# Half of batch 2's q and k taken to their turned form by DMA instead of by TensorE and VectorE

## The chip, the cores and the metric

The kernel runs on one core of one Trainium2 chip. The metric is the device time of one execution in microseconds (us); the time of a kernel is the median of its runs. The engines are called as the profile calls them: PE is TensorE's matmul side, PEld its weight load, DVE is VectorE, ACT is ScalarE, POOL is GpSimd, SP is SyncE, which here only issues DMAs.

## The reference

Eight batches of eight heads, 576 positions, head width 64. `f` is a forget gate per position; its logarithms are summed along the sequence, and the differences of the sums are added to the causal attention scores. The attention output, laid out as 4608 tokens by 512, goes through an MLP.

```python
scores = scale * q @ k^T + (cum[:, :, :, None] - cum[:, :, None, :])   # causal, scale = 1/8
attn = softmax(scores)            # cum = cumsum(log(clip(f, 1e-4, 1)))
x = (attn @ v).transpose(0, 2, 1, 3).reshape(4608, 512)
h = x @ w_in                      # 512 x 2048
out = (h - tanh(h)) @ w_out       # 2048 x 512
```

## The kernel before

All work is in fp16 with fp32 accumulation. The engines' orders are written out by hand: each engine runs its instructions in the order in which the program emits them, and waits in that order.

**Slots.** The work goes by pairs of heads: pair p is batch p // 4, heads 2(p % 4) and 2(p % 4) + 1. Batch 0 has a stage of its own at the start (`scores0`, `values0`). From then on there is one slot per pair, p = 4 to 32 (`slot`, L628). Slot p emits seven score tiles (`scores`, L349, called s0 to s6 here: scores in PE, exponent in ACT, from batch 2 on a causal mask in POOL), the product with v of the pair before it (`values`, L382, after s1), the transposing DMAs of that product's result into XR (`turn`, L400, on SP's queue) and between them a number of MLP steps given by TAKE (L745). An MLP step is four to eight matmuls: `mlp1` gives 128 rows of h for 512 tokens and its gate (ACT tanh L416, DVE add L417), `mlp2` (L577) and `seven` (L520) are the second product. XR is a ring of three batches.

**q and k.** A score needs q and k with the head width on the partitions: QT[b % 2] and KT[b % 2], 64 rows of values and 3 rows that carry the decay (`load_aug`, L168). How they come there differs by batch:

- Batches 1 and 2 (b < FAR, L18): `load_qk` (L213) brings whole rows to the raw tiles qn and kn, six positions to a partition. In slot p, for the pair p + 1, `trans` (L247) makes six PE transposes for q (L256) and two DVE copies to QT (L265), and the same for k (L616 and L620 place them). Each row run is 768 bytes in the raw tile.
- Batches 3 to 7: `load_heads` (L102) brings blocks of 128 positions, five per tensor, with 128 bytes per position and head. `turn_all` (L108) turns the whole tile into TQ or TK by one transposing DMA of 22 blocks of 128 x 128, and `place` (L111) copies from there to QT or KT, one DMA for the even heads (a = 0) and one for the odd ones (a = 1). `turn_all` and `place` are issued by SP, the loads by POOL.

**The table LOADS** (L218 to L238) says after which score tile of which slot a load, a turn or a place is emitted: the key (p, ti) means slot p, behind tile ti. For batch 3 the q loads are in slot 7, the k loads in slot 8, the turn of q at (8, 4), of k at (9, 4), the places of q at (9, 5) and (9, 6), of k at (10, 5) and (10, 6). Slot 12 is the first to use them. v of batch 2 is loaded in slot 5.

So around the change SP's queue holds, in this order: the XR turns of slot 7, a store of the MLP, three decay rows for batch 3 (`load_aug(3)` at (8, 0)), the XR turns of slot 8, a store, the turn to TQ, a store, the XR turns of slot 9, a store, the turn to TK, the places of q, and so on.

**Raw tiles.** Each of qn and kn has two, raw[x][0] for even batches and raw[x][1] for batch 1 and 3; after batch 3 raw[x][1] holds sums of weights for the later MLP. Columns that no load fills must hold finite numbers before a tile is turned; memsets see to that (L155 on DVE at the start, L221 on POOL in slot 5).

Of the kernel before, what the change touches and what calls it, by code (L numbers as in the profile page):

```python
# [14 lines left out]
PITCH = 640  # L15
VW = 66
SHIFT = 5.0
FAR = 3  # L18
# [4 lines left out]
def kernel(  # L23
# [10 lines left out]
    nc = tc.nc  # L34
    P = 128

    B, H, S, D = q.shape
# [4 lines left out]
    NPAIR = H // 2  # L42
    NJ = 5
    AW = D + 4
    NT6 = 6
    RW = H * S * D // (S // NT6)
# [30 lines left out]
    HH = H // 2  # L77
    raw = [[qkp.tile([P, RW], FP16, tag=f"{x}n{i}", name=f"{x}n{i}") for i in range(2)] for x in "qk"]
    qn, kn = ([t[0:S // NT6, :].rearrange("p (h n d) -> p h n d", h=H, n=NT6) for t in ts] for ts in raw)
    qa, ka = (t[0][:, 0:NJ * H * AW].rearrange("p (n h d) -> p n h d", n=NJ, h=H) for t in raw)  # L80
    HP, LEAD = NJ * D, 2 * P
    TC = NPAIR * PITCH + LEAD
# [5 lines left out]
    QT = [qkp.tile([D + 3, H, S], FP16, tag=f"QT{i}", name=f"QT{i}") for i in range(2)]  # L88
    KT = [qkp.tile([D + 3, H, PITCH], FP16, tag=f"KT{i}", name=f"KT{i}") for i in range(2)]
    TQ = qkp.tile([P, TC], FP16, tag="TQ", name="TQ")  # L90
    TK = qkp.tile([P, TC], FP16, tag="TK", name="TK")

    def load_block(dst, src, b, n, h0=0, h1=H):
        pn = min(P, S - n * P)
        nc.gpsimd.dma_start(out=dst[0:pn, n, h0:h1, 0:D], in_=src[b, h0:h1, n * P:n * P + pn, :].rearrange("h p d -> p h d"))  # L95
# [3 lines left out]
        nc.gpsimd.dma_start(out=dst[p0:P, n, :, 0:D],  # L99
                            in_=src[0, :, n * P:(n + 1) * P - p0, :].rearrange("h p d -> p h d"))  # L100

    def load_heads(dst, src, b, n):  # L102
        pn = min(P, S - n * P)
        to = dst[0:pn, n * P:n * P + D]
        to = bass.AP(to.tensor, to.offset, [list(to.ap[0]), [HP, H], [1, D]])
        nc.gpsimd.dma_start(out=to, in_=src[b, :, n * P:n * P + pn, :].rearrange("h p d -> p h d"))  # L106

    def turn_all(dst, src):  # L108
        nc.sync.dma_start_transpose(out=dst.rearrange("p (x t) -> p x t", t=P), in_=src[:, 0:TC])

    def place(dst, src, b, a):  # L111
        of = src[a * D:(a + 1) * D, a * LEAD:a * LEAD + NPAIR * PITCH].rearrange("d (c s) -> d c s", s=PITCH)
        nc.sync.dma_start(out=dst[b % 2][0:D, a:H:2, 0:S], in_=of[:, :, 0:S])

    def load_v(b, n):
        load_block(vn[b % 2], v, b, n)

    def raw_of(b):
        return 1 if b == FAR else 0
# [32 lines left out]
    nc.vector.memset(vn[0][D:P, NJ - 1, :, 0:D], 0.0)  # L152
    nc.vector.memset(KT[0][:, :, S:PITCH], 0.0)
    for one, _ in raw:
        nc.vector.memset(one[3 * P // 4:P, NJ * H * AW:TC], 0.0)  # L155
    first = cst.tile([1, 1], FP32)

    def logs(c0, c1):
# [9 lines left out]
    def load_aug(b):  # L168
        i, h0 = b % 2, b * H
        nc.sync.dma_start(out=KT[i][D:D + 1, :, 0:S], in_=chi[h0:h0 + H, :])  # L170
        nc.sync.dma_start(out=QT[i][D + 2:D + 3, :, :], in_=cq[h0:h0 + H, :])
        nc.sync.dma_start(out=KT[i][D + 1:D + 2, :, 0:S], in_=clo[h0:h0 + H, :])
# [36 lines left out]
    def load_wout(t0, t1):  # L209
        nc.gpsimd.dma_start(out=wout[:, t0:t1, :],  # L210
                            in_=moe_w_out[t0 * P:t1 * P, :].rearrange("(t p) e -> p t e", p=P))

    def load_qk(dst, src, b, h0, h1):  # L213
        nc.gpsimd.dma_start(
            out=dst[b % 2][:, h0:h1, :, :].rearrange("p h n d -> p h (n d)"),
            in_=src[b, h0:h1, :, :].rearrange("h (p n) d -> p h (n d)", n=NT6))

    LOADS = {(NPAIR, 5): [lambda: load_qk(qn, q, 2, 0, H)],  # L218
             (NPAIR, 6): [lambda: load_qk(kn, k, 2, 0, H)]}
    for _, two in raw:  # L220
        LOADS.setdefault((2 * NPAIR - 3, 5), []).append(lambda two=two: nc.gpsimd.memset(two[3 * P // 4:P, 0:TC], 0.0))  # L221
    for i in range(2 * HF):
        LOADS.setdefault((2 * NPAIR + 3 + i // 4, i % 4 * 2), []).append(lambda i=i: weight_sums(i))
    for b in range(2, B):
        p0 = (b - 1) * NPAIR
        for n in range(NJ):
            LOADS.setdefault((p0 + 1, n), []).append(lambda b=b, n=n: load_v(b, n))
        LOADS.setdefault((p0, 0), []).append(lambda b=b: load_aug(b))
        if b < FAR:
            continue  # L230
        for n in range(NJ):
            LOADS.setdefault((p0 - 1, n), []).append(lambda b=b, n=n: load_heads(raw[0][raw_of(b)], q, b, n))
            LOADS.setdefault((p0, n), []).append(lambda b=b, n=n: load_heads(raw[1][raw_of(b)], k, b, n))
        LOADS.setdefault((p0, 4), []).append(lambda b=b: turn_all(TQ, raw[0][raw_of(b)]))
        LOADS.setdefault((p0 + 1, 4), []).append(lambda b=b: turn_all(TK, raw[1][raw_of(b)]))
        for n, (dst, src) in enumerate(((QT, TQ), (KT, TK))):
            for a in range(2):
                LOADS.setdefault((p0 + 1 + n, 5 + a), []).append(lambda b=b, dst=dst, src=src, a=a: place(dst, src, b, a))  # L238
# [194 lines left out]
    def weight_sums(i):  # L433
        what, x = divmod(i, HF // 2)
        lo, hi = slice(2 * x, 2 * x + 2), slice(HF + 2 * x, HF + 2 * x + 2)
        b11, b12, b21, b22 = (wout[:, r, c] for r in (lo, hi) for c in (slice(0, HD), slice(HD, DM)))
        t2x = t2[x // 2][:, x % 2 * 2:x % 2 * 2 + 2, :]
        out, in0, in1 = ((t1[:, lo, :], b12, b11), (t2x, b22, t1[:, lo, :]),
                         (t3[:, lo, :], b22, b12), (tn4[:, lo, :], b21, t2x))[what]
        nc.vector.tensor_tensor(out=out, in0=in0, in1=in1, op=ALU.subtract)  # L440
# [163 lines left out]
    def att_items(p):  # L604
        items = []
        here = pairs[p] if p < len(pairs) else None
        before = pairs[p - 1] if NPAIR < p else None
        after = pairs[p + 1] if p + 1 < len(pairs) else None
        for ti in range(len(TILES)):
            if here:  # L610
                items.append((lambda ti=ti: scores(*here, ti), "s%d" % ti))
            for load in LOADS.get((p, ti), ()):
                items.append((load, ""))
            late = 2 * (p == 2 * NPAIR - 1)
            if ti == late and after and after[0] < FAR:
                items.append((lambda: trans(*after, qn, QT, "AV" if after[0] == 1 else "VV"), "q"))  # L616
            if ti == 1 and before:
                items.append((lambda: (values(*before), turn(*before)), "v"))
            if ti == 3 + late // 2 and after and after[0] < FAR:
                items.append((lambda: trans(*after, kn, KT, "VV"), "k"))  # L620
        return items

# [96 lines left out]
        load_v(1, n)  # L719
    load_qk(qn, q, 1, HH, H)  # L720
    load_qk(kn, k, 1, HH, H)
    for t in range(0, NFT, 4):
        load_wout(t, t + 4)
    scores0(3, 5)
# [54 lines left out]
```

## Time and profile before

| | |
|---|---|
| median of 3 runs | 348.85 us (348.4 to 349.51) |
| the profiled execution | 347.78 us |
| its span, first to last instruction | 346.1 us |
| granted TensorE clock | 0.998 |
| PE busy | 335.8 us (97%) |
| DVE, ACT, POOL busy | 236.3, 222.6, 156.1 us (68%, 64%, 45%) |
| DMA, 16 engines, first 28 of 40 slices | 0.9 or more, nearly all |

The profile is of one execution. A row of the timeline gives the start in us, how long the group took, the engine, the line of the kernel, the operation, out<-in, how often, and in brackets the idle time before it and what ended it. SPq rows are DMA issues: their length is the time that SP spends on the issue, not that of the transfer. Matmuls overlap, so PE's real pace is read from start to start.

Slots can be read from PE's rows: slot 7 begins at 54.4 us, slot 8 at 61.4, slot 9 at 72.9, slot 10 at 83.8, slot 11 at 93.7 and slot 12 at 102.9.

### The profile page before, as it was taken

To read this page: it belongs to the slowest core of one execution; us is meant where nothing else is said; L and a number is where in the kernel's file an instruction comes from. 1 tells how busy PE (TensorE), PEld (TensorE's weight loads), DVE (VectorE), ACT (ScalarE), POOL (GpSimd) and SP (SyncE) were. 2 spreads that over 40 slices of the span, in tenths; PEclk is the share of its full clock that TensorE was granted. 3 is DMA by queue.
4 is the path that set the end of the run, shared out by engine and by line. 5 is a ranking of instruction groups with operands and counts; after the bars stand their busy time and mean duration, and the time that the engine had idled before them with its cause. 6 is when DMAs were issued, how large, how long until landed. Compare 5 with 4: busy or idle time off the path is not lost.

```text
span 346.1 us, 8718 instructions
## 1 busy us (share of the span) xinstructions
PE 335.8 (97%) x3384; PEld 235.9 (68%) x3384; DVE 236.3 (68%) x481; ACT 222.6 (64%) x417; POOL 156.1 (45%) x293
## 2 busy tenths in 40 slices
PE   6889999999999999999999999999999999999995
PEld 3779886555555557888886568656887786486485
DVE  6587888447953598558764885378637865975973
ACT  4777886448755786578757875587568843623631
POOL 8973664655277626664586548652222210000000
PEclk9999999999999999999999999999999999999999
DMA  9999999999999999999999989999330013012002
GB/s 85 139 199 189 204 183 163 157 185 180 166 120 131 203 177 153 120 172 157 172 179 205 163 168 169 196 184 159 81 111 19 17 50 110 0 33 91 0 32 91
DMA packets 161324, 45.96 MB, mean 133 GB/s; under 512 B 141507, under 2 KB 159235, under 8 KB 161283
## 3 DMA queue, kind: packets, MB, share of 16 engines
q0 software_dynamic: 100128, 18.36, 77.2%
q1 hardware_dynamic: 61074, 26.99, 40.0%
q8 instruction: 26, 0.43, 0.5%
q14 instruction: 16, 0.12, 0.1%
q10 hardware_dynamic: 80, 0.07, 0.1%
HBM read 36.85 MB, written 9.44 MB: 134 GB/s over the span
## 4 chain that ended last, share of the span: by engine, by line
PE 87%; DVE 5%; ACT 4%; DMA 2%; issue 1%; ACTq 0%; DVEq 0%
PE hps L464 31%; PE cx L505 14%; PE cz L505 10%; PE ps L360 10%; PE ops L583 8%; PE av L388 7%; PE hps L450 3%; DMA XR<-xn 2%; PE ps L302 1%; ACT e L307 1%; DVE gt L417 1%; DVE KT L265 1%; PE t L274 1%; ACT th L416 1%; ACT e L369 1%
## 5 line engine op out<-in xcount | busy, mean ns | idle before, releaser
L464 PE MATMUL hps<-XR,win 128*128 128x512 f16 (+4 forms) x640 | 125.9, 336 | 1.1 <-DMA XR<-xn 0.8
L417 DVE TENSOR_TENSOR gt<-hps,th 128x512 f16<-128x512 f32 x144 | 98.4, 688 | 39.7 <-ACT th L416 38.5
L369 ACT ACTIVATE e<-ps 128x512 f16<-128x512 f32 x168 | 98.4, 594 | 40.4 <-PE ps L360 37.4
L416 ACT ACTIVATE th<-hps 128x512 f32<-128x512 f32 x144 | 86.1, 598 | 29.8 <-PE hps L464 20.9
L379 POOL TENSOR_SCALAR_AFFINE_SELECT e<-e 128x128 f16<-128x128 f16 x144 | 49.3, 343 | 99.1 <-ACT e L369 98.1
L464 PEld LDWEIGHTS <-win 128*128 128x128 f16 x640 | 56.3, 97 | 43.7 <-issue 0.5
L360 PE MATMUL ps<-QT,KT 67*128 67x512 f16 (+1 forms) x336 | 69.8, 277 | 0.8 <-ACT e L369 0.5
L505 PEld LDWEIGHTS <-gt 128*128 128x128 f16 x560 | 52.5, 97 | 8.3 <-DVE gt L417 0.4
L360 PEld LDWEIGHTS <-KT 67*128 67x128 f16 x336 | 32.2, 98 | 22.7 <-issue 1.4
L95 POOL DMA_DIRECT2D vn<-in_v_dram x40 | 34.1, 856 | 9.9 <-PE ps L363 1.7
L583 PE MATMUL ops<-wout,gt 128*128 128x512 f16 x128 | 32.5, 378 | 0.0
L388 PEld LDWEIGHTS <-e 128*128 128x128 f16 x784 | 28.0, 97 | 3.3
L498 DVE TENSOR_TENSOR snap<-cz,snap 128x512 f32<-128x512 f32 x21 | 14.5, 691 | 22.4 <-PE cz L505 7.4
L388 PE MATMUL av<-vn,e 128*128 128x65 f16 x784 | 29.2, 193 | 0.0
L505 PE MATMUL cz<-wout,gt 128*128 128x256 f16 x224 | 27.8, 272 | 0.0
L106 POOL DMA_DIRECT2D qn<-in_q_dram x25 | 21.2, 850 | 6.0 <-PE ps L363 3.4
L396 DVE TENSOR_TENSOR xn<-av,rs 128x640 f16<-128x640 f32 x28 | 23.1, 825 | 1.0
L505 PEld LDWEIGHTS <-sw 128*128 128x128 f16 x224 | 21.1, 97 | 3.9
L106 POOL DMA_DIRECT2D kn<-in_k_dram x25 | 21.3, 853 | 1.3 <-issue 1.3
L542 ACT ACTIVATE snap<-cx 128x512 f32<-128x512 f32 (+1 forms) x16 | 8.7, 544 | 16.2 <-PE cx L505 16.2
L583 PEld LDWEIGHTS <-gt 128*128 128x128 f16 x128 | 11.0, 97 | 10.0
L307 ACT ACTIVATE e<-ps 128x512 f16<-128x512 f32 x25 | 14.3, 596 | 4.6 <-PE ps L305 2.5
(108 smaller groups left out, 385.6 us busy)
## 6 DMA issues: line engine op xcount, KB each, us to landing
vn<-in_v_dram POOLq DMA_DIRECT2D x32, 128.0 KB, 7.1
out_dram<-ost SPq DMA_DIRECT2D x14, 256.0 KB
out_dram<-snap SPq DMA_DIRECT2D x14, 256.0 KB
qn<-in_q_dram POOLq DMA_DIRECT2D x24, 128.0 KB, 5.3
kn<-in_k_dram POOLq DMA_DIRECT2D x24, 128.0 KB, 4.8
QT<-TQ SPq DMA_DIRECT2D x10, 288.0 KB
KT<-TK SPq DMA_DIRECT2D x10, 288.0 KB
win<-in_moe_w_in_dram POOLq DMA_DIRECT2D x2, 1024.0 KB, 11.1
```

Source lines behind the costliest of these rows:

```text
L95: nc.gpsimd.dma_start(out=dst[0:pn, n, h0:h1, 0:D], in_=src[b, h0:h1, n * P:n * P + pn, :].rearrange("h p d -> p h d"))
L106: nc.gpsimd.dma_start(out=to, in_=src[b, :, n * P:n * P + pn, :].rearrange("h p d -> p h d"))
L360: nc.tensor.matmul(out=ps[:, col:col + n], lhsT=KT[b % 2][0:D + 3, h, j * P:(j + 1) * P], rhs=QT[b % 2][0:D + 3, h, i0:i0 + n], start=True ...
L369: nc.scalar.activation(out=e[:, lo:hi], in_=ps[:, lo:hi], func=AF.Exp, scale=qscale)
L379: nc.gpsimd.affine_select(out=view, in_=view, compare_op=ALU.is_ge, fill=0.0, base=0, pattern=pat, channel_multiplier=-1)
L388: nc.tensor.matmul(out=av[:, a, ib, :], lhsT=E.pop((b, 2 * c + a, j, ib)), rhs=vn[b % 2][:, j, 2 * c + a, 0:D + 1], start=(j == 0), stop=( ...
L396: nc.vector.tensor_tensor(out=xn.rearrange("p i (a d) -> p a i d", a=2), in0=av[:, :, :, 0:D], in1=rs.to_broadcast([P, 2, NJ, D]), op=ALU. ...
L416: nc.scalar.activation(out=th, in_=hps, func=AF.Tanh, scale=-1.0)
L417: nc.vector.tensor_tensor(out=to, in0=view(hps), in1=view(th), op=ALU.add)
L464: nc.tensor.matmul(out=hps[:, o:o + n], lhsT=win[:, ci, ft * P:(ft + 1) * P], rhs=XR[:, ci, t:t + n], start=(ci == 0), stop=(ci == NCH - 1))
L505: nc.tensor.matmul(out=ps, lhsT=stationary(u, LHS[ph], ft, m), rhs=moving(RHS[ph], ft), start=fresh and ft == 0, stop=(ft == HF - 1), skip ...
L583: nc.tensor.matmul(out=ops, lhsT=GT[(u, ft, m)], rhs=wout[:, ft, :], start=(ft == 0), stop=(ft == NFT - 1))
```

## The change

Heads 4 to 7 of batch 2 (pairs 10 and 11) take the way of batches 3 to 7. Pairs 8 and 9 stay with `trans`.

- `load_qk` of batch 2 brings only heads 0 to 3. Heads 4 to 7 come in ten block loads in slot 5, to the free half of the raw tile (column 1536 on).
- Two turns of 12 blocks each: q at (7, 4), k at (8, 1). Four places: both of q at (8, 3), both of k at (8, 6).
- The two `trans` calls of slot 9 and the two of slot 10 go. With two fewer items in each of these slots, the same number of MLP steps is spread over eight items instead of ten.
- v of batch 2 is loaded in slot 6 instead of 5.
- The POOL memsets of raw[x][1] move from slot 5 to the start stage, ahead of the loads of w_out, and cover 768 instead of 2816 columns, in three pieces each; the DVE memset of raw[x][0] covers 352 columns of all partitions instead of 96 of a quarter.

```diff
+    def load_heads(dst, src, b, n, h0=0, o=0):
+        to = dst[0:pn, o + n * P:o + n * P + D]
+        to = bass.AP(to.tensor, to.offset, [list(to.ap[0]), [HP, H - h0], [1, D]])
+        nc.gpsimd.dma_start(out=to, in_=src[b, h0:H, n * P:n * P + pn, :].rearrange("h p d -> p h d"))
+    def turn_all(dst, src, h0=0, o=0):
+        w = (H - h0) // 2 * PITCH + LEAD
+        nc.sync.dma_start_transpose(out=dst[:, 0:w].rearrange("p (x t) -> p x t", t=P), in_=src[:, o:o + w])
+    def place(dst, src, b, a, h0=0):
+        w = (H - h0) // 2 * PITCH
...
+        nc.sync.dma_start(out=dst[b % 2][0:D, h0 + a:H:2, 0:S], in_=of[:, :, 0:S])
...
-        nc.vector.memset(one[3 * P // 4:P, NJ * H * AW:TC], 0.0)
+        nc.vector.memset(one[:, NJ * H * AW:RW], 0.0)
...
-    LOADS = {(NPAIR, 5): [lambda: load_qk(qn, q, 2, 0, H)],
-             (NPAIR, 6): [lambda: load_qk(kn, k, 2, 0, H)]}
-    for _, two in raw:
-        LOADS.setdefault((2 * NPAIR - 3, 5), []).append(lambda two=two: nc.gpsimd.memset(two[3 * P // 4:P, 0:TC], 0.0))
+    LOADS = {(NPAIR, 5): [lambda: load_qk(qn, q, 2, 0, HH)],
+             (NPAIR, 6): [lambda: load_qk(kn, k, 2, 0, HH)]}
+    HW = HH * S * D // (S // NT6)
+    for x, src in enumerate((q, k)):
+        for n in range(NJ):
+            LOADS.setdefault((NPAIR + 1, n), []).append(lambda x=x, src=src, n=n: load_heads(raw[x][0], src, 2, n, HH, HW))
+        LOADS.setdefault((2 * NPAIR - 1 + x, 4 - 3 * x), []).append(
+            lambda x=x: turn_all((TQ, TK)[x], raw[x][0], HH, HW))
+        for a in range(2):
+            LOADS.setdefault((2 * NPAIR, 3 + 3 * x), []).append(
+                lambda x=x, a=a: place((QT, KT)[x], (TQ, TK)[x], 2, a, HH))
...
-            LOADS.setdefault((p0 + 1, n), []).append(lambda b=b, n=n: load_v(b, n))
+            LOADS.setdefault((p0 + (2 if b == 2 else 1), n), []).append(lambda b=b, n=n: load_v(b, n))
...
-            if ti == late and after and after[0] < FAR:
+            if ti == late and after and after < (2, HH // 2):
...
-            if ti == 3 + late // 2 and after and after[0] < FAR:
+            if ti == 3 + late // 2 and after and after < (2, HH // 2):
...
+    for _, two in raw:
+        rows = two[3 * P // 4:P, 0:TC].rearrange("p (s d) -> p s d", d=D)
+        for s0, s1, by in ((NJ - 2, 2 * (NPAIR * NJ + 2), NJ), (1, 2, 1), (NJ * H, NJ * H + 3, 2)):
+            nc.gpsimd.memset(rows[:, s0:s1:by, :], 0.0)
     for t in range(0, NFT, 4):
         load_wout(t, t + 4)
```

## The prediction

> **What bounds the kernel now.** I read the page's first parts and the chain of waits, then the timelines of PE, DVE and SP from 55 to 105 us, then the DMA queues by stage. The chain says that PE's order is the time:
>
> ```profile
> PE 87%; DVE 5%; ACT 4%; DMA 2%; issue 1%; ACTq 0%; DVEq 0%
> ```
>
> So what leaves PE's stream is won, unless PE then waits. The transposes that go stand in slots 9 and 10, and one of the places where the chain leaves PE is there:
>
> ```profile
> 79.07 0.42 PE L256 MATMUL t<-id,kn 96*128 96x96 f16 x6
> 79.33 1.03 PE L464 MATMUL hps<-XR,win 128*128 128x512 f16 x4
> ...
> 82.36 0.38 PE L360 MATMUL ps<-QT,KT 67*128 67x320 f16 x2
> 82.90 1.02 PE L464 MATMUL hps<-XR,win 128*128 128x512 f16 x4 [0.15 <-DVE gt L417]
> 83.76 0.38 PE L360 MATMUL ps<-QT,KT 67*128 67x512 f16 x1
> ```
> ```profile
> 80.51 1.61 DVE L265 COPY KT<-t 64x576 f16<-64x576 f16 x2
> 82.16 2.11 DVE L417 TENSOR_TENSOR gt<-hps,th 128x512 f16<-128x512 f32 x3
> ```
>
> Read the starts: six transposes take PE from 79.07 to 79.33, 0.26 us. Two scores take 0.22 elsewhere (81.28 to 81.50), so at 82.36 the next matmul could start at 82.58; it starts at 82.90, since the gate's add stood behind two copies to KT. That hole is 0.32 us. The last row is slot 10's first score, the first user of what the change moves.
>
> SP's queue decides when that user is served:
>
> ```profile
> 63.33 0.36 SPq L589 DMA_DIRECT2D out_dram<-ost  x1
> ...
> 67.14 1.24 SPq L403 DMA_TRANSPOSE XR<-xn  x1
> 68.42 1.23 SPq L405 DMA_TRANSPOSE XR<-xn  x1
> 69.75 0.53 SPq L589 DMA_DIRECT2D out_dram<-ost  x1
> 70.52 5.33 SPq L109 DMA_TRANSPOSE TQ<-qn  x1
> 75.95 0.53 SPq L589 DMA_DIRECT2D out_dram<-ost  x1
> ```
>
> The turn to TQ holds SP for 5.33 us, and the store behind it goes only at 75.95. SP is full from 63 to 94 us.
>
> **What goes.** Four groups of six transposes at 0.255: 1.02 us of PE, 0.51 in each of slots 9 and 10. Eight DVE copies of 0.80, with them the hole of 0.32 in slot 9 and one of 0.25 in slot 10 (two scores at 92.39, next start 92.86 instead of 92.61, behind the copies at 90.47). Nothing else in these slots is late next: slot 11 has the same matmuls without copies and runs from start to start without a hole. The most there is to win is 1.02 + 0.57 = 1.59 us.
>
> **What is hidden.** Slot 5's two POOL memsets (2.44 each) go. The six that come in their place stand before the loads of w_out, where POOL waits 3.97 us for a DMA (28.5 to 32.48). By 0.44 for 128 x 192 and 2.44 for 2816 columns, a piece costs about 0.3 plus 0.76 ns a column: 2 x (3 x 0.3 + 0.6) = 3.0 us, an estimate, inside the 3.97. The wider DVE memsets, 0.1 before, at most 0.27 each (the row of 67x256), end before the decay's first operation, which waits 0.33 for its DMA. v of batch 2, a slot later, has until slot 9 (75 us).
>
> **The loads.** The halved `load_qk` saves 768 packets of 768 bytes; all 1536 ran from 47.5 to 57.6 in the trace's packet times, so 5 us. The blocks add 4608 packets of 128 bytes; 2716 went in 2.5 us (the stage 59 to 61.5), so 4.2 us. Together nothing: the blocks land at about 59 us. The Trainium skill ("DMA: Bandwidth & Descriptors", Specifications) says that transfers under 512 bytes miss the line rate, which speaks against the blocks. The trace does not bear it out: 0.34 MB in 2.5 us is no slower than 1.18 MB in 10.1.
>
> POOL issues ten loads of about 0.69 for five of 0.86, but five of those move on: slot 7's loads end near 65.5 instead of 62.3. Its masks begin 3 us late; slot 8 leaves POOL 4.7 us free (5.92 busy of 10.6), and they are needed only at 75.3. Cost nothing; without that cover, up to 1 us at the product with v in slot 9.
>
> **The new chain on SP.** A turn of 12 blocks is not in the trace. Below, it is 12/22 of 5.33 = 2.9; above, by the rows of 4 blocks (1.21), 3 x 1.21 = 3.6. I take 2.9, the nearer kind.
>
> - The turn of q fits into SP's idle time, 59.9 to 63.3, if the blocks have landed.
> - The decay rows end at 65.82. The turn of k: to 68.8. XR of slot 8: 2.5, to 71.3 (before 69.65). Its first user is the MLP step at 77.28, and XR's packets ended 1.9 us after the issue: 73.2, no wait. The store: to 72.0. Two places of q, 1.40 as at 86.81: to 73.4.
> - Now a new wait: the turn to TQ for batch 3 overwrites what these places read, so SP stands until they land. Low: the pair issued at 126.22 moved packets from 127.59 to 130.81, half of it is 1.6, so 72.0 + 1.4 + 1.6 = 75.0. High: the store ahead in the queue ended at 74.1 before, moved on by its 2.2 to 76.3, plus 1.6: 77.9. I take 76.4, the middle.
> - The turn to TQ: SP to 81.7; its packets ended 6.9 after the issue (70.52 to 77.42), so 83.3. Behind it the store, 1.0 of packets as at 78.01 to 79.01: 84.3. Then the first place of k, 128 packets, a quarter of 3.2: 85.1. Behind these on SP stand XR of slot 9, a store, the turn to TK and the places for batch 3; XR's user comes after 115 us, and KT of batch 3 lands about 101, its user at 102.9.
>
> **The sum.** Without a wait, slot 10's first score would stand at 83.76 - 0.51 - 0.32 = 82.93. It needs head 4 of KT, the first place of k, at 85.2. PE waits 2.3 us, with all of its stream behind that score. From there slot 10 saves its own 0.51 + 0.25. Net: 85.2 - 83.76 - 0.76 = +0.7 us. By the low ends (75.0, and 5.7 for the turn as at 220.23) the place is there at 82.5 and nothing waits: -1.6. By the high ends (77.9, the 7.9 of 148.69, 1.2 for the place) at 88: +3.5. The profiled execution has 347.78 (346.1 and 1.7 around it) and would come to 348.5; it lies 1.07 under the median, so the median goes from 348.85 to about **349.5**.
>
> **Rivals.**
>
> - *The place is in time* (place of k landed by 82.93): the whole 1.59, 347.3 us. For it: SP's issue times leave 82.5 possible. Against: six transfers in one queue with the loads beside them must all take the short end. The Trainium skill ("Advanced Engine Details and Errata", X-Bar Transpose (TRN2)) says that transposing DMAs are as fast as regular ones; so the turn of k would cost SP what a place does, 0.7, and this rival would hold. In packets the trace agrees (0.72 MB in 2.9 us against 0.59 in 3.2), in SP's time not (5.33 against 1.40). Chance 0.20.
> - *The turns crawl beside the loads*, the way to clearly slower. SP's queue moved far less where POOL's loads were dense than alone:
>
> ```profile
> q0 software_dynamic: 1972, 0.25, 167.4%
> q1 hardware_dynamic: 621, 0.15, 53.1%
> ```
> ```profile
> q1 hardware_dynamic: 2816, 0.72, 110.7%
> q0 software_dynamic: 462, 0.06, 31.1%
> ```
>
>   The first pair is the stage 61.7 to 64.6, the second 74.5 to 77.4; the columns are packets, MB and share. That is 214 against 971 packets a us in SP's queue. A turn's 1536 packets take 1.6 us alone and 7.2 at the first rate. At half that loss per turn the places of q land 4 us later, 80.4, and slot 10 starts at 89: +4.6, 353.4 us. It decides from below about 400 packets a us between 64 and 72 us. Against: in the first pair XR's issue (2.5 us) itself set the pace. Chance 0.15.
> - *Batch 3 pays*: SP is five us behind in slots 9 to 11, and slot 12's first score waits for KT of batch 3, 1 to 2 us beside the forecast: 351. Against: 2 us of room by the sum. Chance 0.12.
> - *The place makes readers of other heads wait*: then slot 8's scores from 70 on wait for the places of q at 76, +6, 355. Against: at 63.63 PE reads heads 0 and 1 of QT while DVE writes 2 and 3 (62.97 to 64.58). Chance 0.04.
>
> **How the numbers follow.** The forecast has 0.45, with its own range of 348.0 to 351.3 (place of k between 83.7 and 87.0); 0.04 is for what I have not seen. A measurement of this kernel tells 0.3%, about 1.05 us, from no change. Faster by more: the first rival, 0.20. Within: two thirds of the forecast and a little of the third rival, 0.36. Slower: the rest, 0.44. The range goes from the first rival, 347.2, to 352.2; above it lie the fourth and most of the second.
>
> **What would show it.** Right: L256 has 72 rows instead of 96; the hole before 82.90 is gone; SP shows a wait between the places of q and the turn to TQ, which starts near 76; PE has one new hole of about 2 us before slot 10's first score, ended by the DMA to KT. Wrong: no hole there (first rival); XR late at 77 or the places after 79 (second); a hole at 103 (third). If POOL's masks end a wait of PE near 75, I costed POOL wrongly.

## The result and the profile after

The changed kernel takes 357.78 us (median of 4 runs, 357.54 to 359.18) against 348.62 (4 runs, 347.87 to 349.51) of the kernel before in the same comparison: a ratio of 1.029, 95% interval 1.026 to 1.033. The prediction was 349.5 with a range of 347.2 to 352.2, so the time lies above the range. The profiled execution took 359.18 us, its span is 357.5, and the granted clock over the span is 0.981 (0.998 before). Ratios here and below leave disturbed runs out, so a few of them are not the quotient of the two medians.

Lines of the helpers lie nine further down than in the kernel before: L369 is the score (L360 before), L473 the first MLP product (L464), L412 and L414 the turns to XR, L110 `turn_all`, L115 `place`. The chain has more DMA in it than before, and the row of the granted clock, in 40 slices of 8.9 us, is not all nines:

```profile
PE 85%; DMA 4%; DVE 3%; issue 3%; ACT 2%; POOL 1%; SPq 1%; ACTq 0%; DVEq 0%; POOLq 0%
```
```profile
PEclk9999999996699999999999999999999999999999
```

The two sixes lie at 80 to 98 us, in slots 9 and 10, where the change is. There PE's timeline has three waits that the kernel before did not have:

```profile
77.39 0.81 PE L473 MATMUL hps<-XR,win 128*128 128x512 f16 x3
79.30 0.38 PE L473 MATMUL hps<-XR,win 128*128 128x512 f16 x1 [1.10 <-DMA XR<-xn]
79.57 1.03 PE L473 MATMUL hps<-XR,win 128*128 128x512 f16 x4
82.53 0.58 PE L369 MATMUL ps<-QT,KT 67*128 67x512 f16 x1 [1.93 <-ACT e L378]
82.91 1.91 PE L473 MATMUL hps<-XR,win 128*128 128x512 f16 x4
...
93.37 0.61 PE L369 MATMUL ps<-QT,KT 67*128 67x512 f16 x1 [3.80 <-DMA KT<-TK]
```

The transposes of `trans` are gone, as they should be. At 77.39 the MLP step finds only three of its four parts of XR. The last row is slot 10's first score: 93.37 instead of 83.76, 9.6 us later. Four matmuls of the MLP take 1.03 us at 79.57 and 1.91 at 82.91: the clock has halved. By stages (columns: stretch, its length, busy time of PE, PEld, DVE, ACT and POOL with counts, granted clock, DMA share, GB/s):

```profile
82.00:88.00 6.00, 5.47 (x15) 2.07 (x15) 2.42 (x4) 4.21 (x9) 3.67 (x7) 0.50 1.75 150
...
92.00:98.00 6.00, 4.63 (x18) 1.94 (x19) 0.69 (x1) 1.82 (x4) 0.59 (x2) 0.50 1.04 204
```

From 82 to 88 PE is busy nearly all the time, but at half the clock.

ACT stood from 75 to 81 for the buffer of a store, and that is what the wait of 1.93 on PE goes back to:

```profile
81.40 0.60 ACT L596 ACTIVATE ost<-ops 128x512 f32<-128x512 f32 x1 [6.07 <-DMA out_dram<-ost]
```

SP's queue, the row of which the prediction made its sum:

```profile
66.51 2.67 SPq L110 DMA_TRANSPOSE TK<-kn  x1
69.28 3.23 SPq L412 DMA_TRANSPOSE XR<-xn  x1
72.56 1.82 SPq L414 DMA_TRANSPOSE XR<-xn  x1
74.48 0.53 SPq L598 DMA_DIRECT2D out_dram<-ost  x1
75.06 1.42 SPq L115 DMA_DIRECT2D QT<-TQ  x2
83.43 4.71 SPq L110 DMA_TRANSPOSE TQ<-qn  x1
...
88.84 1.25 SPq L115 DMA_DIRECT2D KT<-TK  x2
```

SP issues the places of q at 75.06 and stands until 83.43, because the turn to TQ for batch 3 has to wait until they land. Then the turn, a store and the places of k follow; by the trace's packet times the places of k moved from 91.17 to 93.09, and the score starts at 93.37.

Where the 11.4 us of the span (357.5 less 346.1) come from: slot 10's first score is 9.6 us late, of which 0.35 are there at slot 8 already (its first product with v stands at 65.07 against 64.72). Slot 11's first score is 11.3 us late (105.02 against 93.72), and after that the distance stays. So 9.3 us are lost between slot 8 and the place of k, and 1.7 behind it, where slot 10 runs at half clock to 98 us and that costs more than the 0.76 us it saves.

### The profile page after: what moved, and what is told of

It is laid out like the page before. It is cut to its first block, busy times and chain, and to the rows that moved or that the text cites. A ratio compares the mean times of both kernels' runs of the same rounds, so it can differ in the third digit from the quotient of the medians.

```text
span 357.5 us, 8693 instructions
## 1 busy us (share of the span) xinstructions
PE 341.4 (96%) x3360; PEld 237.5 (66%) x3360; DVE 230.2 (64%) x473; ACT 223.0 (62%) x417; POOL 159.8 (45%) x307
## 4 chain that ended last, share of the span: by engine, by line
PE 85%; DMA 4%; DVE 3%; issue 3%; ACT 2%; POOL 1%; SPq 1%; ACTq 0%; DVEq 0%; POOLq 0%
PE hps L473 30%; PE cx L514 13%; PE ps L369 10%; PE cz L514 10%; PE ops L592 7%; PE av L397 7%; PE hps L459 3%; DMA XR<-xn 2%; PE ps L311 1%; PE t L283 1%; DMA KT<-TK 1%; ACT e L316 1%; POOL vn L95 1%; DMA snap<-in_f_dram 1%; PE av L324 1%
## 5 line engine op out<-in xcount | busy, mean ns | idle before, releaser
L473 PE MATMUL hps<-XR,win 128*128 128x512 f16 (+4 forms) x640 | 129.8, 343 | 1.3 <-DMA XR<-xn 1.3
L378 ACT ACTIVATE e<-ps 128x512 f16<-128x512 f32 x168 | 98.5, 594 | 44.5 <-PE ps L369 41.5
L473 PEld LDWEIGHTS <-win 128*128 128x128 f16 x640 | 57.3, 99 | 47.9 <-issue 6.0
L369 PE MATMUL ps<-QT,KT 67*128 67x512 f16 (+1 forms) x336 | 70.9, 281 | 6.8 <-DMA KT<-TK 3.8
L369 PEld LDWEIGHTS <-KT 67*128 67x128 f16 x336 | 32.5, 99 | 29.1 <-issue 4.4
L397 PE MATMUL av<-vn,e 128*128 128x65 f16 x784 | 29.6, 194 | 0.0
L106 POOL DMA_DIRECT2D kn<-in_k_dram x30 | 25.0, 832 | 6.8 <-DMA wout<-in_moe_w_out_dram 2.4
L106 POOL DMA_DIRECT2D qn<-in_q_dram x30 | 24.9, 840 | 6.4 <-DMA wout<-in_moe_w_out_dram 3.0
L403 DVE TENSOR_SCALAR rs<-av 128x10 f32<-128x10 f32 x28 | 4.6, 163 | 21.5 <-PE av L397 21.4
```

What stands on the lines that cost most here:

```text
L106: nc.gpsimd.dma_start(out=to, in_=src[b, h0:H, n * P:n * P + pn, :].rearrange("h p d -> p h d"))
L369: nc.tensor.matmul(out=ps[:, col:col + n], lhsT=KT[b % 2][0:D + 3, h, j * P:(j + 1) * P], rhs=QT[b % 2][0:D + 3, h, i0:i0 + n], start=True ...
L378: nc.scalar.activation(out=e[:, lo:hi], in_=ps[:, lo:hi], func=AF.Exp, scale=qscale)
L397: nc.tensor.matmul(out=av[:, a, ib, :], lhsT=E.pop((b, 2 * c + a, j, ib)), rhs=vn[b % 2][:, j, 2 * c + a, 0:D + 1], start=(j == 0), stop=( ...
L473: nc.tensor.matmul(out=hps[:, o:o + n], lhsT=win[:, ci, ft * P:(ft + 1) * P], rhs=XR[:, ci, t:t + n], start=(ci == 0), stop=(ci == NCH - 1))
```

## The experiments

Times of kernels before are those measured on the same chip with the kernel in question. Slot 10 and slot 12 mean their first scores.

### What there is to win, and the edits priced at nothing

The kernel before with only the moved memsets and v of batch 2 a slot later:

```diff
-        nc.vector.memset(one[3 * P // 4:P, NJ * H * AW:TC], 0.0)
+        nc.vector.memset(one[:, NJ * H * AW:RW], 0.0)
...
-            LOADS.setdefault((p0 + 1, n), []).append(lambda b=b, n=n: load_v(b, n))
+            LOADS.setdefault((p0 + (2 if b == 2 else 1), n), []).append(lambda b=b, n=n: load_v(b, n))
...
+    for _, two in raw:
+        rows = two[3 * P // 4:P, 0:TC].rearrange("p (s d) -> p s d", d=D)
...
```

> The kernel before with only the small edits: memsets trimmed and moved, v of batch 2 a slot later; q and k of batch 2 come as before and are turned by PE. Theory (SP's queue and the loads beside it cost the time): no change, 348.6 within 1.0. Rival (the moved memsets or the later v delay POOL and the loads): slower by 2 or more.

347.5 us (10 runs) against 347.28: 1.001 (0.998 to 1.003). They cost nothing that can be measured.

The same, and the `trans` calls of pairs 10 and 11 taken away with nothing in their place. The part that is left out: heads 4 to 7 of batch 2 get no q and k of their own and are scored with what batch 0 left in QT and KT.

```diff
-            if ti == late and after and after[0] < FAR:
+            if ti == late and after and after < (2, HH // 2):
...
-            if ti == 3 + late // 2 and after and after[0] < FAR:
+            if ti == 3 + late // 2 and after and after < (2, HH // 2):
```

> The kernel of the run with the moves only, without the 24 transposes and 8 copies of pairs 10 and 11, and with nothing in their place: heads 4 to 7 of batch 2 are scored with what QT and KT still hold of batch 0, a part of the computation that is left out. It bounds what the change can win. By the sum 1.59 less, 347.0; if the holes behind DVE come back elsewhere, 1.0 less; if PE's removal is worth nothing, 348.6.

346.07 us (10 runs): 0.996 (0.993 to 0.999), 1.3 us less by this ratio. The trace says it more sharply. These are the first matmuls of the products with v in slots 8 and 11 of the kernel before, and then of this one:

```profile
64.72 0.58 PE L388 MATMUL av<-vn,e 128*128 128x65 f16 x14
...
95.89 0.59 PE L388 MATMUL av<-vn,e 128*128 128x65 f16 x14
```
```profile
63.70 0.58 PE L386 MATMUL av<-vn,e 128*128 128x65 f16 x14
...
93.29 0.59 PE L386 MATMUL av<-vn,e 128*128 128x65 f16 x14
```

From slot 8 to slot 11 it is 31.17 us before and 29.59 here: 1.58 us, against the 1.59 of the prediction. (The first row lies between 63.3 and 65.8 us in the traces of this case, so distances inside a trace are the better measure; the kernel with the moves alone has the same 31.17 as the kernel before.) The win side is right, and the whole of the loss lies with what was put in place.

### Which wait sets the end

The places of k ahead of the turn to TQ:

```diff
-            LOADS.setdefault((2 * NPAIR, 3 + 3 * x), []).append(
+            LOADS.setdefault((2 * NPAIR, 3), []).append(
```

> The changed kernel with both places of k ahead of batch 3's turn to TQ. Theory (slot 10 waits for places that stand behind that turn): the places of k are issued near 77 instead of 88.8, slot 10's first score no longer waits for KT, its 3.8 us of waiting and about half of the slow clock go: 352 to 354. The late store that holds ACT stays, and with it the first hole. Rival (the cost is the DMA engines' load itself, in whatever order): 357 to 358.

351.43 us (4 runs) against 347.28: 1.013 (1.009 to 1.016). More than half of the loss goes. The wait for KT is gone; the two others stay in the timeline, 1.17 us for XR and 1.85 for ACT, and the clock is 0.50 to 0.66 from 82 to 90 us.

The changed kernel with batch 3's k loads, and v of batch 3, a slot later, so that the turn of k and XR of slot 8 have the DMA engines nearly alone:

```diff
...
-            LOADS.setdefault((p0, n), []).append(lambda b=b, n=n: load_heads(raw[1][raw_of(b)], k, b, n))
+            LOADS.setdefault((p0 + (b == FAR), n), []).append(lambda b=b, n=n: load_heads(raw[1][raw_of(b)], k, b, n))
```

> The changed kernel with batch 3's k and v loads a slot later, so that the turn of batch 2's k has none of POOL's loads beside it but the end of batch 3's q. Theory (SP's queue crawls beside dense loads): the turn and XR of slot 8 take about 3 us of packets instead of 7.8, the store that ACT waits for lands before 78, ACT's 6 us wait goes, the places of q land near 76 and slot 10 starts near 85: 349 to 351. Rival (order on SP alone): slot 10 still starts near 91, 355 or more.

354.76 us (4 runs): 1.022 (1.018 to 1.026). The 2112 packets of the turn of k and XR moved from 71.15 to 74.59, in 3.4 us; in the changed kernel they took from 71.42 to 79.19, 7.8 us. The DMA queues between 71.5 and 73.5 us (packets, MB, share of 16 engines), first of the changed kernel, then of this one:

```profile
q0 software_dynamic: 1020, 0.13, 98.5%
q1 hardware_dynamic: 701, 0.18, 68.7%
```
```profile
q1 hardware_dynamic: 844, 0.22, 126.4%
q0 software_dynamic: 40, 0.00, 3.6%
```

XR is no longer late. But the places of q still landed only at 79.79, the turn to TQ went at 80.73, and slot 10 waits as it did:

```profile
89.39 0.61 PE L369 MATMUL ps<-QT,KT 67*128 67x512 f16 x1 [6.34 <-DMA KT<-TK]
```

A third buffer for the stores in the changed kernel, at all four places where the tile is made, so that ACT doesn't wait for one:

```diff
...
-            ost = tmp.tile([P, DM], FP32, tag="ost", name="ost")
+            ost = tmp.tile([P, DM], FP32, tag="ost", name="ost", bufs=3)
```

> The changed kernel with only the third buffer for the stores. ACT's wait of 6.1 us for the store goes, and with it PE's wait of 1.9 for ACT. Theory (the queue ahead of the places of k sets slot 10's start, whatever PE does before it): PE waits longer for KT instead, slot 10 starts at the same 93, total within 1.0 of the changed kernel. Rival (ACT's wait is the cause, the rest follows): 4 or more below the changed kernel.

356.13 us (4 runs) against 347.36: 1.025 (1.022 to 1.028). The wait for ACT has gone from PE, and the one for KT has grown from 3.8 to 6.1 us. Not all of it was slack, though: slots 8 to 11 take 39.42 us in this trace against 42.12 in the changed kernel. With ACT free, POOL issued the last three of batch 3's v loads at 79.69 to 82.78 instead of 83.03 to 85.33, the turn to TQ moved its packets in 3.4 us (86.06 to 89.50) instead of 5.1 (85.29 to 90.38), and the places of k landed at 91.44. That fewer loads beside the turn made it faster is argued, not shown. By the two ratios, the intervals of which overlap a little, it is 1.6 us: more than the theory allowed and far less than the rival's 4.

XR first, that is the turn of k a tile later in the changed kernel:

```diff
-        LOADS.setdefault((2 * NPAIR - 1 + x, 4 - 3 * x), []).append(
+        LOADS.setdefault((2 * NPAIR - 1 + x, 4 - 2 * x), []).append(
```

> The changed kernel with the turn of k issued a tile later, behind XR of slot 8 instead of ahead of it. Theory: the MLP step at 77.4 us no longer waits for XR (1.1 us in the changed kernel), so PE keeps full clock until slot 10; the place of k is as late as before, so 1 to 3 us are won of the 9: 355 to 357. Rival (XR's lateness cost nothing of its own, the place of k sets the time): 357 to 358, the same as the changed kernel.

358.18 us (4 runs) against 347.6: 1.028 (1.022 to 1.034). The rival expectation held: XR's lateness cost nothing of its own that the times show. The wait of 1.10 is gone, and PE waits 8.97 us for the same KT. So the wait for XR was slack in front of the place of k, and the wait for ACT was so in part.

### What the half clock costs

Matmuls that nobody reads, where PE waits in the changed kernel: 8 ahead of slot 9's fifth score tile, 28 ahead of slot 10's first.

```diff
+    def idle_work(n):
+        w = ps_tr.tile([P, UW], FP32, tag="tr", name="w")
+        for _ in range(n):
+            nc.tensor.matmul(out=w, lhsT=ones16[:, 0:P], rhs=ones16[:, 0:UW])
...
+            if (p, ti) in WORK:
+                items.append((lambda p=p, ti=ti: idle_work(WORK[(p, ti)]), ""))
...
```

> The changed kernel with dummy matmuls on PE, 8 ahead of slot 9's fifth score tile and 28 ahead of slot 10's first, where PE idles. They do no work of the reference. Theory (the granted clock of 0.50 follows from PE's idle stretches): the clock stays near 1.0 from 82 to 98 us, slot 10's first steps run at full pace, 2 to 3 below the changed kernel although matmuls were added; the start of slot 10 stays where it is. Rival (the low clock has another cause): clock 0.50 as before and the time the same or longer.

356.0 us (4 runs) against 347.36: 1.025 (1.022 to 1.028). The clock is granted in full in the same stretches:

```profile
82.00:88.00 6.00, 6.00 (x31) 2.82 (x30) 3.92 (x6) 3.97 (x8) 3.44 (x7) 1.00 1.62 174
...
92.00:98.00 6.00, 5.45 (x55) 3.13 (x56) 3.06 (x6) 3.58 (x7) 0.73 (x3) 1.00 1.03 185
```

Slot 10 starts at 92.56, 28.96 us behind slot 8's first product with v, and so no earlier than in the changed kernel (28.30). So the half clock follows from PE's idling, and it is worth some 1.5 to 1.8 us of the 9: 0.004 of 348 by the ratios, the intervals of which overlap a little, and 1.8 by the traces, in which slots 8 to 11 take 40.33 us against 42.12. The Trainium skill ("TensorE: Matmul & The Clock Gate", What's actually happening) has a clock gate that goes to half rate after an idle window of about 3.4 us and back after a busy one. The trace agrees on the half rate (0.50, and 1.91 us for what took 1.03) and on the cause. It does not on how much idling is needed: between 77.4 and 82.5 PE had only waits of 1.10 and 1.93 us with short work between, and of two later kernels one kept 1.00 behind a single wait of 3.17 us and the other fell to 0.50 behind one of 2.78 (XR and the places both first).

### Mending the landings one after another

Five kernels put the above together and move more. The first is places first with batch 3's k loads later; the second adds the third store buffer.

> The changed kernel with both edits of the two runs before: the places of k ahead of the turn to TQ, and batch 3's k and v loads a slot later. Theory (slot 10 waits for nothing but the places of k, and those for the queue ahead of them): the places of k land near 81, before slot 10's first score at 83; no wait for KT, the clock stays full, and what is left is the win of the removed transposes less a short wait of ACT for the late store: 1.0 below the kernel before, at most 0.5 above it. Rival (the block loads and turns cost time by themselves): 2 or more above the kernel before.

356.08 us (6 runs, 351.0 to 358.72) against 347.36: 1.019 (1.014 to 1.025). The profiled run is the fastest of them. In it slots 9 and 10 are as they were meant to be, with full PE and a clock of 1.0 to 100 us (slots 8 to 11 take 29.59 us, as with nothing in place), and slot 12 waits:

```profile
105.14 0.39 PE L369 MATMUL ps<-QT,KT 67*128 67x512 f16 x1 [2.78 <-DMA KT<-TK]
```

This KT is that of batch 3. What the longer executions hold in addition was not traced.

> As the run before, with a third buffer for the tile that ACT fills for the stores of the MLP, so that ACT no longer waits for the late store. Theory: 1.3 below the kernel before, the bound that the run with nothing in place gave; a rival, that the store did not matter: the same as the run before within 0.5.

355.77 us (6 runs): 1.024 (1.021 to 1.027), in the profiled run (352.89) a wait of 4.00 at slot 12. Next, batch 3's four places were issued earlier, ahead of XR of slot 10, in the order QT, KT, QT, KT:

```diff
-        for n, (dst, src) in enumerate(((QT, TQ), (KT, TK))):
-            for a in range(2):
-                LOADS.setdefault((p0 + 1 + n, 5 + a), []).append(lambda b=b, dst=dst, src=src, a=a: place(dst, src, b, a))
+        for a in range(2):
+            for n, (dst, src) in enumerate(((QT, TQ), (KT, TK))):
+                at = (p0 + 1 + n, 5 + a) if b > FAR else (p0 + 1, 6) if n + a == 0 else (p0 + 2, 0)
+                LOADS.setdefault(at, []).append(lambda b=b, dst=dst, src=src, a=a: place(dst, src, b, a))
```

> Kernel after with all three chains shortened: both places of batch 2 ahead of the turn to TQ, batch 3's k and v loads a slot later (so the turn of k and XR of slot 8 run alone), three store buffers, and batch 3's four places issued ahead of the transposed loads of XR of slot 10 in the order QT, KT, QT, KT. Theory (the time is lost only where a head lands after its first score, and PE's idling halves the clock behind it): no wait of PE at slot 10 and none at slot 12, granted clock 1.0 throughout, 1.3 us below before as the kernel with nothing in place, 345.9 to 346.5. First rival (SP's queue as a whole is too full, and what is taken from one wait turns up in another): the first score of slot 12 still waits 2 us or more or XR of slot 10 is late, 351 or more. Second rival (batch 3's turn of k waits for its loads, now a slot later): slot 12 waits as in the two kernels with both moves, 353.

352.59 us (6 runs) against 348.12: 1.012 (1.009 to 1.015). The theory of this run failed: slot 12 waits 5.6 us. The waits of SP's queue between 85 and 110 us (total, how often, longest) hold this line:

```profile
SPq L115 <- DMA TK<-kn: 4.7, 1, 4.7
```

The place of KT waits for the turn to TK. Batch 3's k loads, which it turns, had landed by 85.31; the turn was issued at 91.12, and its packets moved from 94.95 to 100.24, beside the v loads of batch 3 and the q loads of batch 4. Two variants of it, the k loads five tiles later instead of seven, and the loads of batch 3 not moved at all:

```diff
+            LOADS.setdefault(divmod(p0 * 7 + n + 5 * (b == FAR), 7), []).append(lambda b=b, n=n: load_heads(raw[1][raw_of(b)], k, b, n))
```

> The same as the kernel with batch 3's places early, but batch 3's k loads go only five of a slot's seven tiles later. Theory of late landing: the turn to TK no longer waits for its loads, so slot 12 has more room, and no wait at slot 10 if the turn of k and XR are still alone in their queue: 346 to 346.5, not above the kernel with seven tiles. Rival (the turns crawl beside the loads): two of the loads meet the packets of XR of slot 8 again, XR is late by 0.5 to 1.2 us at 77.4 us and the half clock follows: 349 to 352.

354.96 us (6 runs): 1.017 (1.013 to 1.021), with a wait of 6.6 at slot 12.

> Places of batch 2 ahead of the turn to TQ, three store buffers, batch 3's places early; batch 3's loads stay where the change has them. Theory (the loads beside the turn of k and XR are a cause of their own): XR of slot 8 waits 1.2 us as in the changed kernel, ACT no longer waits for the store's buffer, PE goes to half clock for some 6 us or less: 349.5 to 351.5. Rival (the store's buffer was what idled PE there, not XR): no half clock, 347 or less.

352.91 us (6 runs): 1.015 (1.011 to 1.019). XR waits 1.0, as expected; the clock stays at 1.00 around it and slot 10 waits for nothing, but slot 12 waits 2.9, which neither expectation had.

### The shared tile, and XR first

Tiles of their own for the turned half of batch 2, so that the turn to TQ overwrites nothing that the places read:

```diff
+    OWN = [qkp.tile([P, H // 4 * PITCH + LEAD], FP16, tag=f"T{x}2", name=f"T{x}2") for x in "qk"]
...
-            lambda x=x: turn_all((TQ, TK)[x], raw[x][0], HH, HW))
+            lambda x=x: turn_all(OWN[x], raw[x][0], HH, HW))
...
```

> The changed kernel with tiles of their own for the turned half of batch 2, so that batch 3's turn to TQ overwrites nothing that the places still read. Theory (the wait of the turn to TQ for the landed places is what makes the place of k late): the turn to TQ is issued at about 76.5 instead of 83.4, the places of k land about 6 us earlier, near 87, slot 10's first score waits about 4 us less on the clock of the trace, and the kernel comes 3 to 6 us below the changed one, 352 to 355; XR of slot 8 is as late as before that. Rival (the places of k are late because the queue's packets crawl, whatever SP does): they land after 91 as in the changed kernel, 357.

355.71 us (4 runs) against 347.6: 1.022 (1.017 to 1.028). The turn to TQ goes at 77.08, as expected, and here is what becomes of the six us:

```profile
77.08 7.39 SPq L111 DMA_TRANSPOSE TQ<-qn  x1
...
85.15 1.25 SPq L116 DMA_DIRECT2D KT<-Tk  x2
```

The turn holds SP for 7.39 us instead of 4.71, its packets end at 87.68, and the places of k land at 91.53 instead of 93.09. The wait that was removed came back as a longer issue and slower packets: the landing itself is late, not only SP.

Both orders mended, XR before the turn of k and the places of k before the turn to TQ:

> Both orders mended on SP, nothing else: XR of slot 8 ahead of the turn of k, and the places of k ahead of the turn to TQ. Theory (two late landings and the half clock behind them are the whole loss): no wait at 77.4, slot 10 starts within 1 us of 83, the clock stays at 1.0 there; then only slot 12's first score may wait for KT of batch 3, which is set by the turn to TQ at about 83: 346.5 with room, 350 to 352 if it waits. Rival (XR first makes the turn of k so late that its places miss slot 10): slot 10 waits 2 us or more, 352 or above.

353.52 us (4 runs): 1.018 (1.011 to 1.025), with a wait of 2.78 at slot 10. The same with tiles of their own and a third store buffer:

> Tiles of their own for the turned half, XR of slot 8 ahead of the turn of k, places of k ahead of the turn to TQ, three store buffers; the loads stay where the change has them. Theory: no wait at 77.4 or at slot 10, the turn to TQ goes at about 78.5 instead of 83, so KT of batch 3 lands before slot 12's first score: the 1.3 us of the kernel with nothing in place, 346 to 346.7. Rival (SP has no room for the two added turns whatever their order): slot 12's first score waits 2 us or more and PE goes to half clock behind it, 351 or more.

352.25 us (4 runs): 1.012 (1.007 to 1.017). It waits twice:

```profile
87.00 0.39 PE L370 MATMUL ps<-QT,KT 67*128 67x512 f16 x1 [3.17 <-DMA KT<-Tk]
107.61 0.39 PE L370 MATMUL ps<-QT,KT 67*128 67x512 f16 x1 [2.03 <-DMA KT<-TK]
```

The places of k were issued at 81.42, and their first packet moved at 84.94. Between 82 and 84 us the queues show one line:

```profile
q0 software_dynamic: 2448, 0.31, 256.5%
```

That is POOL's loads alone; SP's queue moved nothing. Both expectations of a win had failed by now, and what was left as a cause was the loads.

### The loads left out

The part that is left out in the next two: the ten block loads of q and k of batch 3. Batch 3 is turned from what batch 1 left in the same tiles, whose spare rows are cleared in slot 5 as in the kernel before. First the changed kernel, with every order on SP kept:

```diff
-        for n in range(NJ):
+        for n in range(0 if b == FAR else NJ):
             LOADS.setdefault((p0 - 1, n), []).append(lambda b=b, n=n: load_heads(raw[0][raw_of(b)], q, b, n))
...
+    for _, two in raw:
+        LOADS.setdefault((2 * NPAIR - 3, 5), []).append(lambda two=two: nc.gpsimd.memset(two[3 * P // 4:P, 0:TC], 0.0))
```

> Part left out: the ten block loads of q and k of batch 3 (128-byte packets issued by POOL in slots 7 and 8) are not made; batch 3 is turned from what batch 1 left in the same tiles, and its rows are cleared in slot 5 as in the kernel before. All of the changed kernel's own operations and their order on SP stay. Theory (the turns, the store and the places crawl because these loads share the DMA engines with them): turn of k and XR move in 3.5 us instead of 7.8, places of q land near 78, the turn to TQ goes near 79, place of k lands at 84 to 88 instead of 93, XR does not wait; 349 to 353, some 5 us or more under the changed kernel. Rival (the order on SP and the shared tile set the landing): place of k still lands at 90 or later, 355 to 358.

352.7 us (4 runs) against 347.97: 1.015 (1.010 to 1.021). That is 4.7 us over before, where the changed kernel has 9.2: the loads are about half of the loss. The 2112 packets of the turn of k and XR take 5.4 us (3.5 were expected), the places of q land at 77.68 instead of 82.11, XR is in time. The rest is the order on SP, for slot 10 still waits:

```profile
88.56 0.61 PE L371 MATMUL ps<-QT,KT 67*128 67x512 f16 x1 [6.03 <-DMA KT<-TK]
```

Then the mended order of the kernel with its own tiles, without the loads:

> The same part left out, with own tiles, XR first, places of k first and three store buffers. Theory (with the loads gone and the orders mended nothing is late): no wait at 77.4, at slot 10 or at slot 12, full clock: 345.8 to 346.7, the 1.3 us of the kernel with nothing in place. Rival (SP alone has no room for two more turns): slot 10 or slot 12 still waits 2 us or more, 350 or above.

346.09 us (10 runs) against 347.97: 0.995 (0.993 to 0.997). SP's queue now runs as it was meant to (the places of k at 73.84), and slots 8 to 11 take 29.59 us between the same rows as above, the number of the kernel with nothing in place:

```profile
63.32 0.58 PE L400 MATMUL av<-vn,e 128*128 128x65 f16 x14
...
92.91 0.59 PE L400 MATMUL av<-vn,e 128*128 128x65 f16 x14
```

The 1.58 us are not kept, though. In the profiled run slot 12 still waits for batch 3's KT:

```profile
101.25 0.39 PE L372 MATMUL ps<-QT,KT 67*128 67x512 f16 x1 [1.14 <-DMA KT<-TK]
```

From slot 8 to slot 12 the same products stand 40.10 us apart here, 40.37 in the kernel before and 38.79 with nothing in place. So 0.27 of the 1.58 is left, and the rest of the gain in the ratio comes from elsewhere, perhaps from the missing loads; no run shows from where. What the run does show is that the loss of the changed kernel is gone: SP has room for the two turns and four places up to slot 11, if they are ordered well and the loads are not there, and is about 1 us short at slot 12.

### Half of it

Only q of heads 4 to 7 goes by DMA; k is loaded and turned by PE as before (with batch 3's places early as above):

```diff
-             (NPAIR, 6): [lambda: load_qk(kn, k, 2, 0, HH)]}
+             (NPAIR, 6): [lambda: load_qk(kn, k, 2, 0, H)]}
-    for x, src in enumerate((q, k)):
+    for x, src in enumerate((q,)):
...
-            if ti == 3 + late // 2 and after and after < (2, HH // 2):
+            if ti == 3 + late // 2 and after and after[0] < FAR:
...
```

> Only q of heads 4 to 7 goes by DMA; k of these heads is loaded and turned on TensorE as before; batch 3's places early. Theory: half the transposes go (12 of 24, 0.5 us of PE and part of the holes), the turn of k and the place of k do not exist, so XR of slot 8 is served as before or 1.5 us later at the most and no head is late: 0.3 to 0.7 below before, 346.7 to 347.1. Rival (any added turn on SP in these slots makes a wait): slower than before by over 1 us, with a wait of PE at XR of slot 8 or at slot 10's or slot 12's first score.

347.6 us (12 runs) against 348.12: 0.999 (0.997 to 1.001). PE waits for no DMA from 55 to 130 us and the clock is 1.00. It takes 12 of the 24 transposes out of PE, and leaves SP without the turn and the places of k (2.67 and 1.25 us of issue in the changed kernel). Inside its trace slots 8 to 11 take 30.81 us, 0.36 less than before, and slot 12 keeps it. The run times can't tell a gain this small from none; no kernel that computes everything was measured to beat the kernel before.

## Why the prediction was wrong, point by point

- **What goes: right.** 1.59 us predicted, 1.58 in the trace of the kernel with nothing in place, 1.3 by its ratio.
- **What is hidden: right.** The kernel with the moves alone is within 0.3% of before.
- **The loads: near, but read wrongly.** The last block landed at 61.1 us instead of 59. The 5 us saved were read from a stretch that the 768-byte packets shared with XR; where they ran alone (53 to 55 us of the kernel before) 523 of them moved 0.40 MB in 2 us, so 768 are 2.9 us, an estimate, and the blocks' 4.2 are more than that. Nor do the rows speak for the small packets: they moved 0.14 MB a us (0.34 in 2.5), the larger ones 0.20. What it did to the loads behind the blocks matters more: POOL issued batch 3's q loads from 61.45 to 65.7, where it had issued them from 53.35 to 62.3. The prediction had the 65.5, and priced it for POOL's masks, not for SP's queue, beside which these loads now ran.
- **The turns on SP: near enough in issue time.** 2.9 us each was the estimate; 1.57 and 2.67 were measured. The turn of k ended on SP at 69.2, against 68.8. XR's issue behind it took 5.1 us (3.23 and 1.82) instead of 2.5.
- **The failed step: "XR's packets ended 1.9 us after the issue: 73.2, no wait".** They ended at 79.19. The 1.9 us were read where no turn stood ahead of XR's 576 packets in SP's queue. Here the 1536 of the turn of k did, and the prediction had priced that turn in SP's issue time and put it at nothing in the queue: 2112 packets took 7.8 us, 272 a us, with POOL's loads beside them. The kernel before had a rate for it: beside such loads its XR of slot 8 moved 576 packets from 69.09 to 71.57, 232 a us, by which 1536 more are 6.6 us, an estimate. The turn of q, put down as free, was not free in the queue either: the packets of the decay rows behind it ended at 71.49, 1.8 us later than before. The rest of the chain follows from this: the store landed at 80.87 (76.3 at the high end of the prediction), the places of q at 82.11 (76.4), the turn to TQ went at 83.43 (76.4), and from there on the prediction's own steps hold: 6.95 us from the turn's issue to its last packet (6.9), then a store and the places, both landed at 93.09; the prediction had 85.1 for the first (85.2 in its sum). The leading error is 5.7 us at the places of q, and 1.3 more passed between their landing and the next issue.
- **The rival "the turns crawl beside the loads" was the case**, and its condition, below about 400 packets a us between 64 and 72 us, held just behind that stretch: the turn of q itself still went at 470 (1536 from 64.65 to 67.92), the turn of k with XR at 272 from 71.42 on. In the us from 75 the packets of the two queues come one for one (412 and 413), each at about 31 ns against 18 alone. The size was half: +4.6 predicted, +9.2 measured. The prediction moved the places of q to 80.4 by it; by its own numbers two turns at half the loss (2.8 us each) make 82.0, and 82.11 was measured. It didn't carry the later turn and store through, nor the half clock. A chance of 0.15 was too low: the "against" (XR's issue had set the pace in the one pair of rows) was a guess, and the 232 a us of slot 8's XR, most of whose issue was over by then, spoke against it. The Trainium skill ("DMA: Bandwidth & Descriptors", Queues, rings and completion order) says that each DMA engine goes round between the queues that have work for it; the even split in that us agrees with it. As a price the rule would not have been enough: half of the 971 a us alone would be 486, an estimate, and 272 were measured over the 7.8 us, in which POOL's queue moved 4052 packets to 2207 of SP's.
- **Not seen: a store that holds ACT.** The store behind XR landed at 80.87, and ACT waited 6.07 us for its buffer. Most of this was slack in front of the place of k (with a third store buffer the wait for KT grew by 2.3), but by the ratios 1.6 us of it was not.
- **Not seen: the half clock.** Some 1.5 to 1.8 us of the 9.
- **The rival "batch 3 pays" was no side case but what comes next.** With batch 2's landings mended in whole or in part, slot 12 waits 2.0 to 6.6 us in six kernels, and 1.14 even without the loads.
- **The place in time** came about only where the order on SP was changed. In five kernels slots 8 to 11 then take 29.6 us, and slot 12 took most or all of the gain back; with the places first alone, the waits for XR and ACT and the half clock did.

What was settled: the loss is the late landing of the place of k. By the kernel without batch 3's loads about half of it is POOL's loads in the same DMA engines, and the rest the order on SP; either alone leaves a loss of 1.2% or more, both mended leave none. What stays open: why SP's queue moved no packet for 2 us while POOL's went on (2448 packets), where the trace shows only that it did; what gave the kernel without the loads its ratio; and the scatter of some mended kernels (351 to 359).

## What to carry to other kernels

Before work is moved from a busy engine to a DMA queue, count what else will be in the DMA engines in those very microseconds, the other queue's small packets above all, and take a transfer's time from a row under that load: alone it was 3.4 us, beside the loads 7.8. Then look at what stands behind the new transfers in the same queue, for each of them is late too, and at tiles that the next user overwrites. A gain of 1.6 us bought with 7 us of issue on a queue that is already full (1.57, 2.67, 1.42 and 1.25) has to be right at every landing; half the move, whose landings had room, lost nothing, and gained 0.36 us in its trace, too little for the run times to show.

## What the runs showed of the hardware

- A wait of PE of one to two us, twice within five, was enough for a granted clock of 0.50 for six us; of single waits one of 2.78 was enough in another kernel, and one of 3.17 was not in a third.
- How long a transposing DMA holds SP does not go by its size alone: the 22 blocks to TQ took 3.35 us of issue in one kernel (k loads five tiles later) and 7.39 in another (tiles of their own), the 12 blocks 1.44 (own tiles without batch 3's loads) to 4.29 (XR first).
